# A delta-rule attention and SwiGLU kernel: the first group's triangular inverse by 16-row blocks, two to a partition, with TensorE turning rows and partitions

## The chip, the cores and the metric

The kernel runs on one core of one Trainium2 chip. The core has TensorE (PE, with its weight loads PEld), VectorE (DVE), ScalarE (ACT), GpSimd (POOL) and SyncE (SP, which here only issues DMAs). The metric is the device time of the whole program in microseconds, the median over several runs; lower is better.

## The reference

```python
B, H, S, D = 4, 8, 768, 48
k_n = k / (norm(k) + 1e-6)
for t in range(S):
    kt, vt, bt = k_n[:, :, t], v[:, :, t], beta[:, :, t, None]
    y[:, :, t] = einsum('bhd,bhde->bhe', q[:, :, t], state)
    v_old = einsum('bhde,bhd->bhe', state, kt)
    state += bt[..., None] * einsum('bhd,bhe->bhde', kt, vt - v_old)
x = y.transpose(0, 2, 1, 3).reshape(3072, 384)
out = (silu(x @ w_gate) * (x @ w_val)) @ w_out      # 384 -> 1536 -> 384
```

The first half is a recurrence over 768 steps for each of 32 pairs of batch and head; the second is a feed-forward block (FFN) over all 3072 tokens. The FFN's weights come as float64 and are converted on the chip.

## The kernel before

The sequence is cut into 12 chunks of C = 64 steps. Within a chunk the recurrence is solved in closed form: with A the strictly lower part of the products of K with itself, scaled by beta, the chunk's updates are the inverse of a unit triangular 64x64 matrix (times beta) applied to V minus what the state already holds. Such an inverse is needed for every chunk and each of the 32 pairs of batch and head. Two chunks make a group (6 groups).

The stages, with their functions:

- `norms(c)` (L299 to L326) normalizes K: a square and a sum on DVE (on POOL from chunk 2 on), a power 0.5 on POOL (L314), then an add, a reciprocal and a multiplication. It is a generator, and each `step` runs it to its next `yield`.
- `betas()` (L272) brings beta to partitions with 48 small PE products (p_b), ACT copies and one DVE transpose (L293).
- `turned(c, of_q)` (L328) turns K or Q by eight 128x128 PE transposes into two PSUM banks (p_t), and ACT copies all 1024 columns at once (L337).
- `gram(c, of_q)` (L341) makes the 64x64 products of K with K or with Q, 32 matmuls, and DVE copies them out of PSUM with one multiplication by a mask (L359), to a_sb or p_sb. K's mask also zeroes the upper right 32x32 block and gives the lower left one a minus sign.
- `invert(g)` (L377) inverts the 32x32 diagonal blocks: each of the 128 partitions holds one block, 1024 elements. `turn` (L366) moves a_sb into mb by DVE 32x32 transposes (L369, L372), L393 scales mb by minus beta, then 31 steps of a multiplication (L404, tmp) and an addition (L410, zb) run the substitution, zb is turned back into zt, and six more transposes make z1 (L425, L430).
- `join(g, chunks)` (L434) fills in the off-diagonal 32x32 block with two rounds of 32x32 PE products (p_j, L446 and L461), with an ACT copy between them (L452) and two copies into zt (L465, one on ACT and one on DVE).
- `advance(c)` (L474) uses zt, V and the state to produce the chunk's output and the next state, and turns the output for the FFN (x_ffn).
- `ffn(c, point, fill)` (L562) runs the FFN of a chunk's 256 tokens: six pairs of p_gate and p_val groups (L574), each followed by a silu on ACT (L583) and a product on DVE (L587), then two p_o groups (L595). `point` and `fill` put pieces of the next chunks' work between them.

`convert` (L166) makes float32 out of float64 words for one of 30 weight pieces: five DVE instructions (L178, L190, L199, L208, L217) and one on ACT (L186), which the fourth DVE instruction waits for. The pieces' loads run four ahead on SP's queue (`stage`, L149). `fill` (L702) issues conversions during chunk 0's FFN by a formula over the number done so far, and the rest of them after its last pair; only then do the invert steps of later groups go in.

The order of instructions on each engine is the order of the program text (`tc.manual_schedule`). L733 to L780 is that order: loads, norms of chunks 0 and 1, betas, K's and Q's transposes and products, all of `invert(0)`, then chunk 0's half of `join(0)` and `advance(0)`, with a conversion between every two steps, then the twelve FFN chunks. PSUM tiles come from `ps_pair` (tags px and py, two banks each, one buffer) and `ps_ffn` (tag ffn, four single banks); a tile of a tag waits until the one before it has been read.

Of the kernel before, what the change touches and what calls it, by code (L numbers as in the profile page):

```python
# [8 lines left out]
FP32 = mybir.dt.float32  # L9
# [5 lines left out]
C = 64  # L15
# [6 lines left out]
def kernel(  # L22
# [46 lines left out]
    def ps_pair(name, tag):  # L69

        return psum.tile([128, 2, 512], FP32, name=name, tag=tag, bufs=1)

    def ps_ffn(shape, name):
        return psum.tile(shape, FP32, name=name, tag="ffn", bufs=4)
# [159 lines left out]
    spare = const.tile([128, 1], FP32, name="spare")  # L234
    nc.scalar.activation(spare, half[:, 0:1], ACTF.Silu)


    mask_k = const.tile([128, C], FP32, name="mask_k")
    mask_q = const.tile([128, C], FP32, name="mask_q")
    for m in (mask_k, mask_q):  # L240
        nc.gpsimd.memset(m, 1.0)
        for b in range(2):
            rows = m[64 * b : 64 * b + 64]
            nc.gpsimd.affine_select(
                out=rows,
                in_=rows,
                compare_op=ALU.is_ge,
                fill=0.0,
                base=-1,
                pattern=[[1, C]],  # L250
                channel_multiplier=-1,
            )
    for b in range(2):
        nc.gpsimd.memset(mask_k[64 * b : 64 * b + R, R:C], 0.0)
        nc.gpsimd.memset(mask_k[64 * b + R : 64 * b + C, 0:R], -1.0)

    state = const.tile([128, 2, NB, NJ, D], FP32, name="state")
    beta_b = const.tile([128, NG, R], FP32, name="beta_b")
# [4 lines left out]
    def half_of(x):  # L263
        return slice(64 * x, 64 * x + 64)
# [34 lines left out]
    def norms(c):  # L299
# [25 lines left out]
            load_k(c + 2)  # L325
        yield  # L326

    def turned(c, of_q, tag=None):  # L328

        x = qpad[c % QB] if of_q else knp[c % AHEAD]  # L330
        xt = work.tile([128, NB, NJ, 2, C], FP32, name="qt" if of_q else "kt", bufs=AHEAD)
        (qt if of_q else kt)[c] = xt
        p_t = ps_pair("p_t", tag or ("py" if of_q else "px")).rearrange("p bp (j n) -> p bp j n", j=NJ)
        for bp in range(NB):
            for j in range(NJ):
                nc.tensor.transpose(p_t[:, bp, j], x[:, bp, 2 * j : 2 * j + 2], ident)  # L336
        nc.scalar.copy(xt.rearrange("p bp j b i -> p bp j (b i)"), p_t)  # L337
        if of_q and c + QB < NCH:
            load_q(c + QB)

    def gram(c, of_q, tag=None):  # L341

        xt = (qt if of_q else kt)[c]
        p_g = ps_pair("p_g", tag or ("py" if of_q else "px")).rearrange("p par (bp j i) -> p par bp j i", bp=NB, j=NJ)
        for bp, j, par, b, _ in every():
            nc.tensor.matmul(  # L346
                p_g[half_of(b if of_q else b ^ par), par, bp, j],
                kt[c][half_of(par), bp, j, b],
                xt[half_of(par), bp, j, b],
            )  # L350
        if of_q:
            p_sb[c] = work.tile([128, 2, NB, NJ, C], FP32, name="p_sb", bufs=AHEAD)
            dst = p_sb[c].rearrange("p par bp j i -> p (par bp j) i")
        else:
            g = c // 2
            if c % 2 == 0:
                a_sb[g] = work.tile([128, 2, HH, C], FP32, name="a_sb")
            dst = a_sb[g][:, c % 2]
        nc.vector.tensor_tensor(  # L359
            out=dst,  # L360
            in0=p_g.rearrange("p par bp j i -> p (par bp j) i"),
            in1=(mask_q if of_q else mask_k)[:, None, :].to_broadcast([128, HH, C]),
            op=ALU.mult,
        )

    def turn(out, in_):  # L366

# [6 lines left out]

    z1s = {}

    def invert(g):  # L377

        mb = work.tile([128, R, R], FP32, name="mb", bufs=1)
        zb = work.tile([128, R, R], FP32, name="zb", bufs=1)  # L380
        nc.gpsimd.memset(zb, 0.0)
        nc.gpsimd.tensor_copy(
            zb.rearrange("p k i -> p (k i)")[:, 0 : R * R : R + 1], beta_b[:, g]
        )
        nbeta = work.tile([128, R], FP32, name="nbeta")
        nc.gpsimd.tensor_scalar_mul(nbeta, beta_b[:, g], -1.0)
        a_v = a_sb[g].rearrange("p c h i -> p i (c h)")
        z_v = ztp[g % ZB].rearrange("p c h i -> p i (c h)")
        yield from turn(
            lambda rows, half: mb[rows].rearrange("p j i -> p i j"),  # L390
            lambda rows, half: a_v[rows, R * half : R * half + R],
        )
        nc.vector.tensor_tensor(  # L393
            out=mb,
            in0=mb,
            in1=nbeta[:, None, :].to_broadcast([128, R, R]),
            op=ALU.mult,
        )
        yield
        for j in range(R - 1):  # L400
            m = R - 1 - j
            tmp = work.tile([128, 256], FP32, name="tmp", bufs=1)
            t_v = tmp[:, 0 : (j + 1) * m].rearrange("p (k i) -> p k i", i=m)
            nc.vector.tensor_tensor(  # L404
                out=t_v,
                in0=zb[:, 0 : j + 1, j : j + 1].to_broadcast([128, j + 1, m]),
                in1=mb[:, j : j + 1, j + 1 : R].to_broadcast([128, j + 1, m]),
                op=ALU.mult,
            )
            nc.vector.tensor_tensor(  # L410
                out=zb[:, 0 : j + 1, j + 1 : R],
                in0=zb[:, 0 : j + 1, j + 1 : R],
                in1=t_v,
                op=ALU.add,
            )
            yield
        yield from turn(
            lambda rows, half: z_v[rows, R * half : R * half + R],
            lambda rows, half: zb[rows].rearrange("p k i -> p i k"),
        )  # L420

        z1 = work.tile([128, 2, NJ * NB, R], FP32, name="z1", bufs=1)
        zt = ztp[g % ZB].rearrange("p c (m e) i -> p c m e i", e=2)
        for c in range(2):
            nc.vector.transpose(z1[:, c], zt[:, c, :, 0, 0:R])  # L425
        yield
        for s in range(2):
            hi, lo = slice(64 * s, 64 * s + R), slice(64 * s + R, 64 * s + C)
            for c in range(2):
                nc.vector.transpose(z1[lo, c], zt[hi, c, :, 1, 0:R])  # L430
            yield
        z1s[g] = z1

    def join(g, chunks=slice(0, 2)):  # L434

        zt, a, z1 = ztp[g % ZB], a_sb[g], z1s[g]
        n = chunks.stop - chunks.start
        M = HH // 2
        p_j = ps_pair("p_j", "px")[:, 0].rearrange("p (c m i) -> p c m i", c=2, m=M)
        for c in range(chunks.start, chunks.stop):  # L440
            for m in range(M):
                for e in range(2):
                    for s in range(2):
                        lo = slice(64 * s + R, 64 * s + C)
                        dst = slice(64 * s + R * e, 64 * s + R * e + R)
                        nc.tensor.matmul(  # L446
                            p_j[dst, c, m],
                            a[lo, c, 2 * m + e, 0:R],
                            zt[lo, c, 2 * m + e, R:C],
                        )  # L450
        t2 = work.tile([128, 2, M, R], FP32, name="t2", tag="tmp", bufs=1)
        nc.scalar.copy(t2[:, chunks], p_j[:, chunks])  # L452
        yield
        p_j = ps_pair("p_j", "py").rearrange("p e (c m i) -> p e c m i", c=2, m=M)
        for c in range(chunks.start, chunks.stop):
            for m in range(M):
                for e in range(2):
                    for s in range(2):
                        row = slice(64 * s + R * e, 64 * s + R * e + R)
                        hi = slice(64 * s, 64 * s + R)  # L460
                        nc.tensor.matmul(p_j[hi, e, c, m], z1[row, c, m], t2[row, c, m])  # L461
        zt_v = zt.rearrange("p c (m e) i -> p e c m i", e=2)
        for s, copy in ((0, nc.scalar.copy), (1, nc.vector.tensor_copy)):
            hi = slice(64 * s, 64 * s + R)
            copy(  # L465
                zt_v[hi, :, chunks, :, R:C].rearrange("p e c m i -> p e (c m) i"),
                p_j[hi, :, chunks].rearrange("p e c m i -> p e (c m) i"),
            )
        yield
# [254 lines left out]
    with tc.manual_schedule(  # L724
# [13 lines left out]
        nc.gpsimd.memset(ztp[0], 0.0)  # L738
        for c in (0, 1):
            step("norm", norms, c)  # L740
        step("betas", betas)
        step("norm", norms, 0)
        turned(0, False)
        step("norm", norms, 1)
        turned(1, False, "py")
        step("betas", betas)
        gram(0, False)
        gram(1, False, "py")

        turned(0, True)  # L750
        turned(1, True)
        for _ in invert(0):
            pass
        gram(0, True)
        one = join(0, slice(0, 1))
        load_v(1)
        next(one)
        converts(1)
        next(one)
# [49 lines left out]
```

## Time and profile before

| | us |
|---|---|
| median of 3 runs (815.23 to 817.8) | 815.56 |
| profiled execution, whole | 817.87 |
| profiled execution, span | 816.2 |
| PE busy | 719.5 |
| PEld busy | 573.6 |
| DVE busy | 430.8 |
| ACT busy | 145.0 |
| POOL busy | 80.5 |
| first p_gate of the FFN starts at | 83.35 |
| last weight conversion ends at | 158.4 |

The span runs from the first to the last instruction of the profiled execution, and the positions in this text are microseconds from its start. An instruction's row in the order of time gives its start, its duration, the engine, the line, the operation, the tiles and shapes (partitions x elements), and in brackets how long the engine was idle before it and what ended the wait. A row with x2 merges several. A small float32 matmul appears as two records on PE and two weight loads on PEld, so x64 is 32 matmuls; a 128x128 transpose is one record. The granted clock is the share of PE's full clock that its throttle let through.

### The profile page before, as it was taken

Reading aid. Unit: us, or ns where it says so; the run is one execution under the profiler, and the core shown is the slowest. Engines: PE = TensorE matmul, PEld = TensorE weight load, DVE = VectorE, ACT = ScalarE, POOL = GpSimd, SP = SyncE. Lnnn points to the kernel's source line nnn. Section 1 sums busy time; section 2 is a strip of 40 time slices with the busy share of each in tenths; the row PEclk is TensorE's granted clock in tenths of the full one; section 3 lists DMA queues with packets and bytes.
Section 4 is the critical chain, followed back from the end, with each engine's and each line's share of the span. In section 5 each row is a group of like instructions: output and inputs, shape, how many; then the busy total and the mean of one; then the engine's idle time right before and its main releaser. Section 6 shows DMA issues by size and latency. Waiting matters only on the chain.

```text
span 816.2 us, 20536 instructions
## 1 busy us (share of the span) xinstructions
PE 719.5 (88%) x9384; PEld 573.6 (70%) x9384; DVE 430.8 (53%) x768; ACT 145.0 (18%) x230; POOL 80.5 (10%) x73
## 2 busy tenths in 40 slices
PE   3304868399989999999999999999999999999997
PEld 2303757268758877868868868868868778688784
DVE  3899799849824785207881157852277511011010
ACT  2003223311012111121201211211202111021110
POOL 6000032122003020030110121100000000000000
PEclk9655899599998999999999999999999999999999
DMA  8604564412013120120210211001001000000000
GB/s 192 110 1 105 174 174 110 132 31 50 0 25 58 22 49 12 22 49 15 44 23 12 40 31 31 2 21 22 2 20 22 2 21 2 10 12 1 19 1 19
DMA packets 85094, 34.45 MB, mean 42 GB/s; under 512 B 78064, under 2 KB 81136, under 8 KB 85008
## 3 DMA queue, kind: packets, MB, share of 16 engines
q1 hardware_dynamic: 79008, 27.93, 14.9%
q10 hardware_dynamic: 6000, 5.21, 2.7%
q8 instruction: 73, 1.20, 0.6%
q14 instruction: 13, 0.11, 0.0%
HBM read 28.41 MB, written 4.72 MB: 41 GB/s over the span
## 4 chain that ended last, share of the span: by engine, by line
PE 77%; DVE 15%; issue 4%; DMA 2%; POOL 1%; ACT 1%; ACTq 0%; POOLq 0%; DVEq 0%
PE p_gate L574 22%; PE p_o L595 21%; PE p_val L574 21%; PE p_g L346 2%; PE p_t L336 2%; DVE mant L199 2%; DVE power L208 2%; DVE zb L410 1%; DVE tmp L404 1%; PE p_u L505 1%; PE p_y L535 1%; DVE mant L190 1%; PE p_s L522 1%; PE p_r L484 1%; PE p_y L493 1%
## 5 line engine op out<-in xcount | busy, mean ns | idle before, releaser
L574 PE MATMUL p_gate<-x_ffn,wg_sb 128*128 128x256 f32 x864 | 205.7, 388 | 0.0
L574 PE MATMUL p_val<-x_ffn,wv_sb 128*128 128x256 f32 x864 | 198.7, 379 | 0.5 <-DVE wv_sb L217 0.5
L595 PE MATMUL p_o<-wo_sb,h_f 128*128 128x384 f32 x576 | 191.1, 490 | 0.0
L574 PEld LDWEIGHTS p_val<-x_ffn,wv_sb 128*128 128x128 f32 x864 | 164.0, 190 | 23.4 <-DVE wv_sb L217 1.2
L574 PEld LDWEIGHTS p_gate<-x_ffn,wg_sb 128*128 128x128 f32 x864 | 161.6, 192 | 23.6 <-DVE wg_sb L217 0.5
L587 DVE TENSOR_TENSOR h_f<-sil,p_val 128x512 f32<-128x512 f32 x72 | 49.3, 685 | 226.7 <-PE p_val L574 226.6
L595 PEld LDWEIGHTS p_o<-wo_sb,h_f 128*128 128x128 f32 x576 | 108.9, 191 | 72.7 <-issue 0.9
L583 ACT ACTIVATE sil<-p_gate 128x512 f32<-128x512 f32 x72 | 43.0, 597 | 211.2 <-PE p_gate L574 192.0
L410 DVE TENSOR_TENSOR zb<-zb,tmp 128x31 f32<-128x31 f32 (+15 forms) x186 | 68.5, 368 | 6.4
L404 DVE TENSOR_TENSOR tmp<-zb,mb 128x31 f32<-128x31 f32 (+15 forms) x186 | 67.8, 364 | 5.0
L314 POOL TENSOR_TENSOR norm<-norm,half 128x16 f32<-128x16 f32 x12 | 35.4, 2953 | 165.4 <-DVE norm L308 163.6
L603 ACT COPY o_sb<-p_o 128x384 f32<-128x384 f32 x24 | 11.5, 480 | 202.7 <-PE p_o L595 202.7
L318 POOL TENSOR_TENSOR kn<-kin,norm 128x768 f32<-128x768 f32 x10 | 14.8, 1479 | 293.6 <-DVE norm L317 246.6
L359 DVE TENSOR_TENSOR a_sb<-p_g,mask_k 128x1024 f32<-128x1024 f32 x12 | 14.7, 1223 | 45.2 <-PE p_g L346 45.2
L346 PE MATMUL p_g<-kt 64*64 64x64 f32 x768 | 16.1, 244 | 19.1 <-ACT kt L337 19.1
L446 PE MATMUL p_j<-zt,a_sb 32*32 32x32 f32 x768 | 8.3, 197 | 26.2 <-DVE zt L369 26.2
L346 PEld LDWEIGHTS p_g<-kt 64*64 64x64 f32 x768 | 14.5, 156 | 23.2 <-ACT kt L337 19.6
L186 ACT ACTIVATE power<-power,rebias 128x512 int32<-128x512 uint32 (+1 forms) x30 | 19.9, 677 | 58.4 <-DVE power L178 56.2
L446 PEld LDWEIGHTS p_j<-zt,a_sb 32*32 32x32 f32 x768 | 7.5, 108 | 28.8 <-issue 28.7
L372 DVE STREAM_TRANSPOSE zt<-zb 32x1024 f32<-32x1024 f32 x12 | 26.3, 2188 | 0.1
L372 DVE STREAM_TRANSPOSE mb<-a_sb 32x1024 f32<-32x1024 f32 x12 | 25.6, 2136 | 0.3
L465 DVE COPY zt<-p_j 32x1024 f32<-32x1024 f32 (+1 forms) x7 | 7.5, 1070 | 32.3 <-ACT zt L465 32.2
(85 smaller groups left out, 548.1 us busy)
## 6 DMA issues: line engine op xcount, KB each, us to landing
wo_sb<-in_moe_w_gate_dram SPq DMA_DIRECT2D x9, 512.0 KB, 3.6
wo_sb<-in_moe_w_val_dram SPq DMA_DIRECT2D x9, 512.0 KB, 3.8
qpad<-in_q_dram SPq DMA_DIRECT2D x48, 96.0 KB, 3.0
vin<-in_v_dram SPq DMA_DIRECT2D x96, 48.0 KB, 2.4
out_dram<-o_sb ACTq DMA_DIRECT2D x48, 96.0 KB, 2.2
kin<-in_k_dram SPq DMA_DIRECT2D x44, 96.0 KB, 2.9
staged<-in_moe_w_out_dram SPq DMA_DIRECT2D x6, 384.0 KB, 3.2
zt<-in_moe_w_out_dram SPq DMA_DIRECT2D x6, 384.0 KB, 3.6
```

Source lines behind the costliest of these rows:

```text
L186: nc.scalar.activation(power.bitcast(I32), power, ACTF.Relu, bias=rebias, scale=8.0)
L199: nc.vector.scalar_tensor_tensor(out=mant.bitcast(FP32), in0=words[:, :, 0], scalar=2.0**-32, in1=mant, op0=ALU.mult, op1=ALU.add,)
L208: nc.vector.scalar_tensor_tensor(out=power, in0=words[:, :, 1], scalar=0x80000000, in1=power, op0=ALU.bitwise_and, op1=ALU.bitwise_or,)
L314: nc.gpsimd.tensor_tensor(out=norm, in0=norm, in1=half, op=ALU.pow)
L346: nc.tensor.matmul(p_g[half_of(b if of_q else b ^ par), par, bp, j], kt[c][half_of(par), bp, j, b], xt[half_of(par), bp, j, b],)
L372: nc.vector.transpose(out(rows, 0), in_(rows, 0))
L404: nc.vector.tensor_tensor(out=t_v, in0=zb[:, 0 : j + 1, j : j + 1].to_broadcast([128, j + 1, m]), in1=mb[:, j : j + 1, j + 1 : R].to_broad ...
L410: nc.vector.tensor_tensor(out=zb[:, 0 : j + 1, j + 1 : R], in0=zb[:, 0 : j + 1, j + 1 : R], in1=t_v, op=ALU.add,)
L574: nc.tensor.matmul(ps[name][:, i], w_sb[:, t, (f + i) * 128 : (f + i + 1) * 128], x[:, t], start=(t == 0), stop=(t == KT - 1),)
L583: nc.scalar.activation(sil, ps[name], ACTF.Silu)
L587: nc.vector.tensor_tensor(out=hs[-1][:, f % 4 : f % 4 + 2], in0=sil, in1=ps["p_val"], op=ALU.mult)
L595: nc.tensor.matmul(p_o, hs[f // 4][:, f % 4, bp * 128 : (bp + 1) * 128], wo_sb[:, f], start=(f == 0), stop=(f == FT - 1),)
```

## The change

Only the first group is treated anew; `invert` remains for groups 1 to 5.

- The new `invert_first(0)` takes the place of `invert(0)`. a_sb reaches mb by 128 small PE products with the identity (p_m) and one DVE multiplication out of PSUM. The diagonal blocks are of 16 rows, two of them side by side in each partition, so the substitution has 15 steps in place of 31. PE turns the blocks back twice (p_z, as they are needed in zt, and p_d, as weights), 16x16 off-diagonal blocks come from two rounds of 128 PE products (p_j), and PE makes z1 (p_1) in place of DVE's transposes.
- `between(n)` puts other work into it: a weight conversion beside p_m (n = 0), Q's transposes and chunk 0's product with Q (n = 1), that product's masks (n = 2), and a conversion each at n = 3 and 4. Before, Q's transposes and product stood around `invert(0)`, and its mask followed it.
- K's mask is gone: K's products are copied as they are (on DVE; chunk 1's on ACT), and the minus sign is put in by `join`'s ACT instruction instead (`scalar.mul` by -1).
- `turned` and `gram` now work with single banks: each copy out of PSUM is two of half the size, in every chunk.
- The two steps of chunk 0's `norms` run before those of chunk 1, on DVE too.
- mb and zb are 1056 elements wide (were 1024). `join(0)`'s first half swaps its PSUM tags. `load_v(1)` is issued ahead of Q's second loads.

```diff
-    mask_k = const.tile([128, C], FP32, name="mask_k")
...
+            nc.scalar.copy(xt[:, bp].rearrange("p j b i -> p (j b i)"), p_t[bp])
...
+            else:
+                at = slice(par * HH // 2, (par + 1) * HH // 2)
+                copy(a_sb[c // 2][:, c % 2, at], p_h)
...
+    def invert_first(g, between):
+        mb, zb, nbeta = blocks(g)
+        a, zt = a_sb[g], ztp[g % ZB]
+        a_v, z_v = (t.rearrange("p c h i -> p (c h) i") for t in (a, zt))
...
+        for j in range(R):
+            for quad, at in QUADS:
+                nc.tensor.matmul(
+                    p_m[quad, R * j : R * j + R], a_v[quad, :, at + j], ident[quad, quad]
+                )
+        between(0)
+        nc.vector.tensor_tensor(
+            out=mb[:, 0 : R * R].rearrange("p (j i) -> p j i", i=R),
+            in0=p_m.rearrange("p (j i) -> p j i", i=R),
+            in1=nbeta[:, None, :].to_broadcast([128, R, R]),
+            op=ALU.mult,
+        )
+        between(1)
+        r = R // 2
...
+        for j in range(r - 1):
+            m = r - 1 - j
+            shape = [128, 2, j + 1, m]
...
+            nc.vector.tensor_tensor(
+                out=t_v,
+                in0=z_h[:, :, 0 : j + 1, j : j + 1].to_broadcast(shape),
+                in1=m_h[:, :, j : j + 1, j + 1 : r].to_broadcast(shape),
+                op=ALU.mult,
+            )
+            done = z_h[:, :, 0 : j + 1, j + 1 : r]
+            nc.vector.tensor_tensor(out=done, in0=done, in1=t_v, op=ALU.add)
...
+        for i in range(R):
+            for quad, _ in QUADS:
+                nc.tensor.matmul(
+                    p_z[quad, R * i : R * i + R], z_t[quad, :, i], ident[quad, quad]
+                )
+        between(2)
+        for n, (quad, at) in enumerate(QUADS):
+            (nc.scalar.copy if n < 2 else nc.vector.tensor_copy)(
+                z_v[quad, :, at : at + R],
+                p_z[quad].rearrange("p (i h) -> p h i", h=2 * HH),
+            )
...
+                nc.tensor.matmul(
+                    p_d[quad, R * k : R * k + R], z_t[quad, k], ident[quad, quad]
+                )
...
+        nc.scalar.copy(d_v, p_d)
...
+                nc.tensor.matmul(
+                    p_j[quad, h],
+                    a_v[quad, h, at : at + R],
+                    z_v[quad, h, at + r : at + R],
+                )
...
+        nc.scalar.mul(t1, p_j, -1.0)
+        between(3)
...
+                nc.tensor.matmul(p_j[quad, h], d_v[quad, h], t1[quad, h])
+        for n, (quad, at) in enumerate(QUADS):
+            rows = slice(quad.start, quad.start + r)
+            (nc.scalar.copy if n % 2 == 0 else nc.vector.tensor_copy)(
+                z_v[rows, :, at + r : at + R], p_j[rows]
+            )
+        between(4)
...
+                        nc.tensor.matmul(
+                            p_1[dst, c, m], zt[hi, c, 2 * m + e, 0:R], ident[hi, hi]
+                        )
+        z1s[g] = work.tile([128, 2, HH // 2, R], FP32, name="z1", bufs=1)
+        nc.scalar.copy(z1s[g], p_1)
...
-        nc.scalar.copy(t2[:, chunks], p_j[:, chunks])
+        nc.scalar.mul(t2[:, chunks], p_j[:, chunks], -1.0)
...
         for c in (0, 1):
             step("norm", norms, c)
+            step("norm", norms, c)
         step("betas", betas)
-        step("norm", norms, 0)
         turned(0, False)
-        step("norm", norms, 1)
         turned(1, False, "py")
         step("betas", betas)
         gram(0, False)
-        gram(1, False, "py")
-
-        turned(0, True)
-        turned(1, True)
-        for _ in invert(0):
-            pass
-        gram(0, True)
-        one = join(0, slice(0, 1))
+        gram(1, False, "py", nc.scalar.copy)
         load_v(1)
+
+        first_q = gram_steps(0, True, "ffn")
+
+        def between(n):
+            if n == 1:
+                for c in range(2):
+                    turned(c, True, "ffn")
+                next(first_q)
+            elif n == 2:
+                next(first_q)
+            else:
+                converts(1)
+
+        invert_first(0, between)
+        one = join(0, slice(0, 1), ("py", "px"))
```

## The prediction

> **What bounds the kernel now.** I read the page's first three parts, then sums over stretches of the span, then the instructions in order of time up to 190 us. The page:
>
> ```profile
> PE 719.5 (88%) x9384; PEld 573.6 (70%) x9384; DVE 430.8 (53%) x768; ACT 145.0 (18%) x230; POOL 80.5 (10%) x73
> PE   3304868399989999999999999999999999999997
> DVE  3899799849824785207881157852277511011010
> PEclk9655899599998999999999999999999999999999
> ```
>
> Over the whole span PE is the bound; in the first eight slices of 20.4 us it is not, and DVE is. The stretches (length, then PE, PEld, DVE, ACT, POOL busy, granted clock, DMA share, GB/s) say it in numbers:
>
> ```profile
> 24.24:65.40 41.16, 6.12 (x144) 5.19 (x144) 38.70 (x77) 2.40 (x3) 1.47 (x1) 0.53 0.27 48
> 65.35:158.40 93.05, 57.91 (x999) 49.51 (x1002) 87.31 (x169) 31.94 (x51) 11.52 (x6) 0.78 0.53 152
> 160.40:816.20 655.80, 644.39 (x7940) 508.95 (x7932) 293.54 (x508) 106.45 (x168) 53.05 (x39) 0.99 0.11 21
> ```
>
> From 24.2 to 65.4 only DVE works (the first group's inverse). From 65.4 to 158.4 DVE is 94% busy, with the 30 weight conversions. From 160.4 on PE is 98% busy. So the time is about (end of the conversions) + 658, and the end of the conversions is DVE's own sum. DVE time taken out ahead of it moves everything behind it. The first group, in order of time:
>
> ```profile
> 24.26 2.14 DVE L369 STREAM_TRANSPOSE mb<-a_sb 128x1024 f32<-128x1024 f32 x1
> 26.44 4.25 DVE L372 STREAM_TRANSPOSE mb<-a_sb 32x1024 f32<-32x1024 f32 x2
> 30.80 1.23 DVE L393 TENSOR_TENSOR mb<-mb,nbeta 128x1024 f32<-128x1024 f32 x1
> 32.05 0.19 DVE L404 TENSOR_TENSOR tmp<-zb,mb 128x31 f32<-128x31 f32 x1
> ...
> 43.26 0.43 DVE L404 TENSOR_TENSOR tmp<-zb,mb 128x256 f32<-128x256 f32 x1
> ...
> 55.41 2.18 DVE L369 STREAM_TRANSPOSE zt<-zb 128x1024 f32<-128x1024 f32 x1
> 57.49 4.31 DVE L372 STREAM_TRANSPOSE zt<-zb 32x1024 f32<-32x1024 f32 x2
> 57.74 1.08 PE L446 MATMUL p_j<-zt,a_sb 32*32 32x32 f32 x64 [26.20 <-DVE zt L369]
> 61.84 0.77 DVE L425 STREAM_TRANSPOSE z<-zt 128x256 f32<-128x256 f32 x2
> 62.64 1.54 DVE L430 STREAM_TRANSPOSE z<-zt 32x256 f32<-32x256 f32 x4
> 64.21 1.23 DVE L359 TENSOR_TENSOR p_sb<-p_g,mask_q 128x1024 f32<-128x1024 f32 x1
> 68.19 0.69 DVE L465 COPY zt<-p_j 32x512 f32<-32x512 f32 x1
> ```
>
> No idle stands between the DVE rows up to 65.4; the last row, at 68.9, completes chunk 0's inverse, with one conversion behind it of 30.
>
> **The change, step by step.** Times are of the profiled execution (span 816.2, whole 817.87; the median of the runs is 815.56). I sum a saving there and take it off the median.
>
> 1. Norms. Chunk 1's square and sum now stand behind chunk 0's power on DVE. Chunk 0's normalized K is ready 1.6 us earlier, which helps nobody, as PE takes both chunks in order. Chunk 1: chunk 0's power ends at 10.39, then 0.16 + 0.25 + 0.96 on DVE, square and sum 1.9, to 13.85, against 12.1 before. So +1.75, and K's products end at 24.7, not 22.93. The copies out of PSUM lose the mask; chunk 1's go to ACT as two halves (0.57 each by a 128x512-like row; half of kt's 1.01 is the other end), against one 1.23 pass on DVE. a_sb is ready at **25.95** (before 24.23).
>
> 2. Rows to partitions: 128 matmuls of 32x32 in place of 6.5 us of transposes. The only 32x32 rows are p_b (48 in 1.50) and p_j: 32 (64 records) in 1.08, or 33.8 ns each, at granted clock 0.5, and 0.75, or 23.4 ns, at 79.6 us. PE has worked from 19 us on here, and in the old trace the 128x128 transposes go from 1.97 to 1.09 us per eight after such a stretch (24.3 us), so 23.4: 3.0 us (cold 4.3). The first conversion runs on DVE beside it. Scaling from PSUM 1.23 (L359's row), and 0.5 (0 to 1.2) for GpSimd's 1.47 us square, which lands at 28.6 as before and has delayed DVE's two-operand rows by about 1.2 us elsewhere (L404 at 188.2 took 1.45). To **30.75**.
>
> 3. The recurrence: 30 instructions, not 62. From the rows, start to start is 0.20 us + 1.02 ns per element (0.23 at 31, 0.46 at 256). The new ones hold 2720 elements: 6.0 + 2.8 = 8.8 us, where 23.4 were. Their four-dimensional views I cost at nothing: the old 1-wide and 31-wide forms take the same 0.2. Q's transposes, copies and product now run on PE and ACT beside the loop (3 to 6 us, ample cover of 8.8). To **39.55**.
>
> 4. Blocks back. 60 of p_z's 128 matmuls go with the loop; 68 are behind it, cold, 2.3 us: 41.85. Q's masks (1.4) hide here. Four 32x1024 copies: two on ACT (1.01), then two on DVE (1.22), one behind the other, since the instruction order shows DVE's wait for ACT: 46.4. Side by side they would end at 44.3, with PE then late at 45.55. PE's p_d (128, 3.7) and ACT's copy of it hide there. They read PSUM 32 elements apart; L369 reads 64 apart at 2.1 ns an element, where the contiguous L293 transpose takes 1.9, so I add nothing, and up to half of 4.5 as the other end.
>
> 5. Joining halves: p_j 128 matmuls 3.2 to 49.65, t1 0.65 to 50.3, the second 128 3.3 to 53.6, four 16-row copies in turn (0.57, 0.69, twice, with 0.05 each) to **56.3**.
>
> 6. Then DVE has two conversions (68.91 to 71.65: 2.74 each) ahead of its zt copy: 61.85, and 62.55 with the copy. p_1 (64 matmuls, 1.9), z1 and join's two products on PE end at 60.2 and ACT's copy at 60.8: covered. Without that cover, slower PE shows at once, 1 for 1.
>
> So zt is whole at 62.55, not 68.88: **6.3 us earlier**. And four conversions are behind it, not one (one beside p_m, one beside the joining, two after): three times 2.74 is 8.2. Until the first p_gate the stages are the same. In the first FFN pairs DVE still decides: PE waits there for p_sb (101.15), wg_sb (104.76), wv_sb (108.09), and the fill's formula then issues three conversions in the first four fills in place of six. DVE's wait of 3.3 us at 86.3 (ACT's L186 stands behind sil, which waits for the first p_gate) stays. Walking pairs 0 to 3 with these rows, DVE comes 7 to 8.8 us sooner to chunk 1's update, counted from the first p_gate; I take **8.0**. The rest to 158.4 and PE's 658 shift unchanged.
>
> Other edits at nothing: later groups' copies as two halves add some 0.15 us per tile to ACT and DVE, both under half busy from 160 us on, where PE is the cover; bounds -1 and +1 us. V's loads now issue ahead of Q's second ones on SP's queue; Q's chunks 2 and 3 are first read past 135 us. GpSimd loses mask work that was done by 4.5 us.
>
> Sum: 6.3 + 8.0 = 14.3; 815.56 - 14.3 = **801.3**.
>
> **A rule that speaks against it.** The weights of p_m, p_z and the second joining product are read 32 or 64 elements apart, 324 such matmuls on the path; every stationary operand in this trace is contiguous, so nothing shows what that costs. The nearest rows give 23.4 (no cost) and twice that (the 64-column p_u, 61 ns cold against 33.8): +7.6 us. I take nothing, as the record count and the width, which set those rows, are the same. The Trainium skill, "SBUF — State Buffer", section "Door 1: The DMA port swizzle", says that fp32 read further than four elements apart leaves its 16-byte line each time and pays for it. It gives no figure; by it the step would be dearer, and by the rows it is free.
>
> **Rivals.**
> - *Strided weights cost double*: 14.3 - 7.6 = 6.7, **808.9**. For it: nothing measured. Against it: L369's 2.1 ns is on DVE, not PE. 10%.
> - *The three hidden conversions are worth nothing*, because PE becomes the bound in the first FFN chunk: only 6.3 stays, **809.3**. For it: PE is 15 of 20 us busy from 100 to 120. Against it: 35 us of PE idle in the 93, 18 of them at one wait at 156.84. 8%.
> - *More*: PE warm throughout, copies side by side (-2.2) and the first p_gate, 5.0 us at 83.4, at the 2.86 of the next, for which DVE now waits 3.3: **797**. 9%.
> - *Slower*: strided weight loads do not overlap the matmul ahead of them. Place: those 324; price: one PEld record of 104 ns (L446's median) in place of 30, +24 us, so **825**. It decides from about 75 ns a matmul on (14.3/324 = 44 more). For it: no row excludes it. Against it: PEld busy is 0.97 of 1.08 us for 64 records, so loads are pipelined. 5%.
> - *It moves nothing*: the weight transfers bound the tail. The last pieces land 0.7 us (153.71 against 154.38) ahead of use, so a slightly later transfer would show, but DVE waits for none today: 815, 2%.
> - The forecast: 66%.
>
> **Numbers.** All cold PE adds 3.4, strided copies 2.3, the later stages 1: 14.3 - 6.7 = 7.6, or 808. The other ends give 797, and 795 with everything. I set 796 to 810, which takes in all but the last two cases and the edge of the others. Faster by over 0.3% (2.4 us, about what a measurement here can tell from no change): 66 + 10 + 8 + 9 = 93%; within 2%; slower 5%.
>
> **What would show it.** Right: DVE's loop near 9 us and ending near 40; the group of 128 matmuls at 3 to 4.3 us; zt whole near 62.5 with three further conversions done; conversions ending near 144; from there 658. Wrong: 128-matmul groups at 6 us or more (strided), a PE stall between the copies, DVE waiting for ACT or PE between 80 and 144, or a PE-bound part longer than 659.

## The result

The changed kernel takes **838.72 us** (median of 4 runs, 836.01 to 846.47) against 815.39 for the kernel before: ratio 1.0296, 95% interval 1.0225 to 1.0367. That is slower by 3%, where 801.3 was forecast, and it lies outside the range of 796 to 810. The profiled execution took 838.62, its span 836.9.

The page of the changed kernel, the lines that answer to those shown of before:

```profile
PE 746.9 (89%) x10792; PEld 595.2 (71%) x10792; DVE 406.3 (49%) x750; ACT 155.1 (19%) x263; POOL 80.0 (10%) x66
PE   2754886489988999989999999999999999999997
DVE  3535899748833876216883137761186711011010
PEclk9855799599998999999999999999999999999999
```

DVE lost 24.5 us of busy time, as intended. In slices 2 to 4 (20.9 to 83.7 us) it is no longer full; PE is not either. The two stretches that matter, in the same columns as in the prediction (length, then PE, PEld, DVE, ACT, POOL busy, granted clock, DMA share, GB/s). The weight conversions end at 158.67 us, as good as unchanged (158.35 before). The first row is the first group of the changed kernel, the second its stretch behind the conversions, the third that same stretch before the change:

```profile
26.00:65.00 39.00, 24.85 (x1259) 22.45 (x1260) 17.60 (x44) 8.18 (x12) 1.76 (x1) 0.65 0.37 72
158.80:836.90 678.10, 653.12 (x8064) 513.45 (x8064) 295.82 (x529) 110.49 (x188) 55.09 (x40) 0.99 0.11 21
158.35:816.20 657.85, 646.44 (x8016) 510.94 (x8008) 294.77 (x510) 106.45 (x168) 55.10 (x40) 0.99 0.11 21
```

In the first one DVE works 17.6 of 39 us and PE 24.9: the stage is now a chain in which each waits for the other. The stretch behind the conversions was 657.85 us before and had been carried over "unchanged". Counted from 158.67 (the row starts 0.13 behind it) it is 678.2, **20.4 longer**, with only 6.7 more PE busy time. So there are two misses, and they add up. Within the profiled executions the forecast was 817.87 - 14.3 = 803.6; the conversions end 14.6 later than the 144.05 that this meant, the rest takes 20.4 more, and 803.6 + 35.0 = 838.6, the time of the profiled execution.

**Miss one, the later stage.** Each turning of K or Q is eight transposes, four into each of the two PSUM banks of one tile. PE in order of time, the turning of K and Q in the changed kernel (chunk 6; start, duration, what runs, in brackets the wait ahead of it):

```profile
300.73 0.60 PE L338 MATMUL p_t<-ident,kn 128*128 128x128 f32 x4
302.00 0.66 PE L338 MATMUL p_t<-ident,kn 128*128 128x128 f32 x4 [0.68 <-ACT kt L339]
302.50 0.60 PE L338 MATMUL p_t<-ident,qpad 128*128 128x128 f32 x4
303.82 0.66 PE L338 MATMUL p_t<-ident,qpad 128*128 128x128 f32 x4 [0.73 <-ACT qt L339]
304.32 7.91 PE L715 MATMUL p_o<-wo_sb,h_f 128*128 128x384 f32 x24
```

and the same place before:

```profile
292.27 1.04 PE L336 MATMUL p_t<-ident,kn 128*128 128x128 f32 x8
293.14 1.04 PE L336 MATMUL p_t<-ident,qpad 128*128 128x128 f32 x8
294.01 7.91 PE L595 MATMUL p_o<-wo_sb,h_f 128*128 128x384 f32 x24
```

From the first transpose to p_o it was 1.74 us and is 3.59. ACT's copy of bank 0 now stands between the two fours, and the second four, which write bank 1 of the same tile, wait for it. Six of the ten later chunks lose 1.85 each, 11.1. Chunks 5 and 7 lose 2.6 and 3.1 (in chunk 7 the wait for ACT's copy is 1.91, not 0.68). Chunks 2 and 3, whose transposes stand elsewhere, lose 3.3 and 2.0: chunk 2's p_g starts at 160.42, not 156.84, of which 0.3 is the later end of the conversions, and chunk 3 takes 5.0 from p_t to p_g, not 3.0. The sum is 22.1, 1.7 more than the 20.4 by which the stage is longer; e5 shows a gain of about that size.

**Miss two, the first group.** PE there, the rows of p_m and then from the first product of p_d on:

```profile
27.05 3.83 PE L413 MATMUL p_m<-ident,a_sb 32*32 32x32 f32 x238 [1.19 <-ACT a_sb L370]
32.83 0.52 PE L413 MATMUL p_m<-ident,a_sb 32*32 32x32 f32 x18 [1.95 <-issue]
...
45.36 0.63 PE L462 MATMUL p_d<-ident,zb 32*32 32x32 f32 x28
47.35 1.93 PE L462 MATMUL p_d<-ident,zb 32*32 32x32 f32 x128 [1.36 <-issue]
51.35 1.54 PE L462 MATMUL p_d<-ident,zb 32*32 32x32 f32 x98 [2.07 <-issue]
...
54.95 1.90 PE L472 MATMUL p_j<-zt,a_sb 32*32 32x16 f32 x128 [1.71 <-issue]
58.41 1.57 PE L472 MATMUL p_j<-zt,a_sb 32*32 32x16 f32 x101 [1.55 <-issue]
60.68 0.63 PE L483 MATMUL p_j<-t,mb 32*32 32x16 f32 x27 [0.70 <-ACT t L478]
62.14 2.01 PE L483 MATMUL p_j<-t,mb 32*32 32x16 f32 x128 [0.83 <-issue]
67.24 1.66 PE L483 MATMUL p_j<-t,mb 32*32 32x16 f32 x101 [3.09 <-issue]
```

Within a row of p_d or p_j a product (two records) takes 30 ns, near the 25 to 29 that these terms were priced at. Between the rows PE stands for 0.8 to 3.1 us, and "issue" says that nothing in the profile released it. From p_d on the rows break every 128 records, right across the steps (28, 128, then 98 of p_d and some 27 of p_j, 128, and so on); p_m ran 238 records before its one pause. 64 products are 128 matmul records and 128 weight loads. The page's part on queues has the answer, queue q8, with packets, MB and share:

```profile
q8 instruction: 84, 1.38, 0.7%
```

1.38 MB in 84 packets is 16.4 KB each; over the 256 instructions of such a row that is 64 bytes each. The counts of whole runs agree: PE and PEld together have 2 x 10792 instructions, which is 84.3 times 256, and before the change 2 x 9384, which is 73.3 times 256, for 73 packets. In the trace of packets one starts 1.0 to 1.7 us after each of these rows has begun in most cases (2.8 us in the row ahead of the longest pause), takes about 0.95 us, and PE resumes 1.3 to 1.5 us after its end. So a burst of small products runs at the pace at which its instructions are brought in: about 3.5 us for 64 products, 54 ns each, not 30.

### The profile page after: what moved, and what is told of

Read it like the earlier page. It is cut to its first block, busy times and chain, and to the rows that moved or that the text cites. A ratio compares the mean times of both kernels' runs of the same rounds, so it can differ in the third digit from the quotient of the medians.

```text
span 836.9 us, 23384 instructions
## 1 busy us (share of the span) xinstructions
PE 746.9 (89%) x10792; PEld 595.2 (71%) x10792; DVE 406.3 (49%) x750; ACT 155.1 (19%) x263; POOL 80.0 (10%) x66
## 3 DMA queue, kind: packets, MB, share of 16 engines
q8 instruction: 84, 1.38, 0.7%
## 4 chain that ended last, share of the span: by engine, by line
PE 78%; DVE 10%; issue 6%; ACT 3%; POOL 2%; DMA 1%; ACTq 0%; POOLq 0%; DVEq 0%
PE p_gate L694 22%; PE p_o L715 21%; PE p_val L694 20%; PE p_g L349 2%; PE p_t L338 2%; DVE mant L199 2%; DVE power L208 2%; PE p_u L625 1%; PE p_y L613 1%; PE p_s L642 1%; PE p_r L604 1%; PE p_y L655 1%; ACT kt L339 1%; DVE mant L190 1%; POOL norm L308 1%
## 5 line engine op out<-in xcount | busy, mean ns | idle before, releaser
L530 DVE TENSOR_TENSOR zb<-zb,tmp 128x31 f32<-128x31 f32 (+15 forms) x155 | 57.9, 374 | 5.3
L524 DVE TENSOR_TENSOR tmp<-zb,mb 128x31 f32<-128x31 f32 (+15 forms) x155 | 57.1, 369 | 3.9
L338 PE MATMUL p_t<-ident,kn 128*128 128x128 f32 x96 | 18.0, 318 | 34.4 <-ACT kt L339 28.9
L370 DVE COPY a_sb<-p_g 128x512 f32<-128x512 f32 x22 | 14.2, 685 | 56.4 <-PE p_g L349 56.4
L338 PEld LDWEIGHTS p_t<-ident,kn 128*128 128x128 f32 x96 | 12.5, 160 | 39.7 <-ACT kt L339 32.0
L338 PE MATMUL p_t<-ident,qpad 128*128 128x128 f32 x96 | 17.4, 318 | 7.2 <-ACT qt L339 7.2
L621 DVE TENSOR_TENSOR vin<-vin,p_r 128x768 f32<-128x768 f32 x11 | 10.5, 954 | 24.0 <-PE p_r L604 23.6
L383 DVE STREAM_TRANSPOSE zt<-zb 32x1024 f32<-32x1024 f32 x10 | 22.0, 2197 | 0.1
L383 DVE STREAM_TRANSPOSE mb<-a_sb 32x1024 f32<-32x1024 f32 x10 | 21.4, 2136 | 0.3
```

What stands on the lines that cost most here:

```text
L338: nc.tensor.transpose(p_t[bp][:, at], x[:, bp, 2 * j : 2 * j + 2], ident)
L383: nc.vector.transpose(out(rows, 0), in_(rows, 0))
L524: nc.vector.tensor_tensor(out=t_v, in0=zb[:, 0 : j + 1, j : j + 1].to_broadcast([128, j + 1, m]), in1=mb[:, j : j + 1, j + 1 : R].to_broad ...
L530: nc.vector.tensor_tensor(out=zb[:, 0 : j + 1, j + 1 : R], in0=zb[:, 0 : j + 1, j + 1 : R], in1=t_v, op=ALU.add,)
```

## The experiments

Kernels measured together share the runs of the kernel before, whose median lay at 815.5 to 816.2 us.

**e1: both copies behind all eight transposes.** The changed kernel with one line more:

```diff
                 nc.tensor.transpose(p_t[bp][:, at], x[:, bp, 2 * j : 2 * j + 2], ident)
+        for bp in range(NB):
             nc.scalar.copy(xt[:, bp].rearrange("p j b i -> p (j b i)"), p_t[bp])
```

> The changed kernel, but in every chunk both half copies of K's and Q's transposes come after all eight transposes, not one between the two fours. Theory A (the copy in the middle makes PE wait before the second four, since the second bank's transposes wait for the reading of the first): the waits of PE for kt and qt inside the transposes go. In the trace of the changed kernel K's and Q's transposes of a later chunk take 3.59 us together where they took 1.74 before, 1.85 us for each of ten chunks, so about 838.7 - 18.5 = 820. Rival (the half-size copies of the products on DVE, or more ACT instructions, make the later stage longer): no change, 837 to 840. Theory B (the first group's gain is eaten by PE waiting for its instructions): what is left over the kernel before is the first group's, so not under 814.

Measured: 815.18 (10 runs) against 815.88, ratio 0.9992 [0.9972, 1.0012]: 23.5 us less than the changed kernel. PE no longer waits inside the eight, and the rest behind the conversions is 654.3 us:

```profile
290.04 1.04 PE L338 MATMUL p_t<-ident,kn 128*128 128x128 f32 x8
290.91 1.04 PE L338 MATMUL p_t<-ident,qpad 128*128 128x128 f32 x8
```

```profile
159.60:813.90 654.30, 644.23 (x8020) 509.32 (x8012) 295.85 (x530) 107.66 (x186) 55.26 (x40) 1.00 0.11 22
```

The place of the copy, not its halving, costs the time. That it fell below the expected 820 is mostly the reckoning: 18.5 was ten times 1.85, and the ten turnings had cost 22.1. The conversions still end at 159.6: miss two is untouched.

**e2: the split alone.** The kernel before, with one half copy inside the loop, and nothing else of the change:

```diff
                 nc.tensor.transpose(p_t[:, bp, j], x[:, bp, 2 * j : 2 * j + 2], ident)
-        nc.scalar.copy(xt.rearrange("p bp j b i -> p bp j (b i)"), p_t)
+            nc.scalar.copy(xt[:, bp].rearrange("p j b i -> p (j b i)"), p_t[:, bp])
```

> The kernel before with one edit: the copy of the transposes is split into two halves, each after its four transposes, as in the change. Theory A: ten chunks by 1.85 us in the later stage and up to 2 more in the first, so 815.4 + 18.5 = 834 (832 to 838). Rival (the split itself is harmless, something else of the change made the later stage longer): 815 to 817.

Measured: 841.64 against 815.88, 1.0297 [1.0273, 1.0322]. This one line alone is enough for the whole slowdown; the length behind the conversions (from 157.1 us) is 680.4:

```profile
157.10:837.50 680.40, 654.59 (x8065) 514.30 (x8064) 294.67 (x510) 110.51 (x188) 55.13 (x40) 0.99 0.11 21
```

It is more than the 832 to 838 expected, which again reckoned 1.85 for each chunk. The stretch is 2.3 longer than in the changed kernel, which has the products' copies split as well (e5).

**e10: the same two fours into two tiles.** Why does bank 1 wait for a copy of bank 0? In the changed kernel, K's fours of the later chunks get a tile each; Q's stay as they are:

```diff
-        p_t = banks("p_t", tag or ("py" if of_q else "px"))
+        if c > 1 and not of_q:
+            p_t = [ps_pair("p_t0", "px")[:, 0], ps_pair("p_t1", "py")[:, 0]]
+        else:
+            p_t = banks("p_t", tag or ("py" if of_q else "px"))
```

> The changed kernel with one edit: from chunk 2 on, K's two fours of transposes write two separate PSUM tiles (bank 0 of tag px, bank 0 of tag py) in place of the two banks of one tile; Q's stay in one tile. If the wait between the fours comes from the tile being one object (theory), K's second four follows the first at once in all ten later chunks (no wait for the kt copy inside K's eight, which now take about 1.04 us), while Q's fours still wait 0.7 us in eight chunks; Q's first four, whose tile now follows K's second one, may wait instead until ACT has read it (about 0.7 us), so the whole time is not the point and may stay at 836 to 840. If the wait comes from PSUM itself (PE kept out while ACT reads), K's second four still waits 0.68 us.

Measured (one run): 841.8, and at the same place:

```profile
302.17 1.04 PE L341 MATMUL p_t<-ident,kn 128*128 128x128 f32 x8
303.94 0.66 PE L341 MATMUL p_t<-ident,qpad 128*128 128x128 f32 x4 [0.73 <-ACT kt L342]
305.27 0.66 PE L341 MATMUL p_t<-ident,qpad 128*128 128x128 f32 x4 [0.68 <-ACT qt L342]
```

K's eight run through; Q's, in one tile, still wait in the middle (and once more ahead, because their tile is now the one that K's second four used). So the wait belongs to the tile, which is one object however many banks it has: the instructions are made to wait for each other by tile, and PSUM itself does not keep PE out. The first group's Q in the changed kernel says the same: its halves are two tiles of the ffn tag, and its 16 transposes run in one row of 3.00 us. The Trainium skill, "PSUM — Partial Sum Buffer", section "PSUM bank collisions raise a hardware error", states that two engines on different banks do not collide and that guarding by bank is enough; these rows agree, since ACT's copy of one tile's bank (from 302.81 on) and PE's writes to the other's (up to 303.21) ran side by side here.

**e3: bursts of small products, measured by themselves.** The kernel before with three bursts of 256 products behind its last: 32 columns with contiguous weights, 32 columns with weights 12 elements apart, 128 columns.

```diff
+        b_w = wo_sb[:, 0].rearrange("p (a b) -> p b a", b=12)
+        for kind in range(3):
+            p_x = ps_pair("p_x" + str(kind), ("px", "py", "px")[kind])[:, 0]
+            for i in range(256):
+                quad = slice(32 * (i % 4), 32 * (i % 4) + 32)
+                if kind == 1:
+                    w = b_w[quad, i // 4 % 12]
+                else:
+                    w = wo_sb[quad, i // 4 % 12, 0:32]
+                n = 128 if kind == 2 else 32
+                nc.tensor.matmul(p_x[quad, 0:n], w, ident[quad, 0:n])
```

> The kernel before with three bursts of 256 PE products added behind its last one, which nothing reads: 32x32 weights contiguous, 32 columns moving; the same with weights read 12 elements apart; 32x32 weights contiguous with 128 columns moving. The data transfers are nearly over by then. Theory B (small products use up instructions faster than they are brought: 128 records, with their loads 256 instructions, per block of 16 KB): the first two bursts run alike, in stretches of 128 records at 23 to 34 ns a product with a pause of 1.3 to 2 us between that has no releaser, about 3.5 us per 64 products; the third, at some 200 ns a product, has no pause. Rival (strided weights load slower): the second burst is slower than the first within the stretches, by 20 ns a product or more. Rival (PSUM or row groups pace the products): no pauses, but 50 ns or more a product in both.

Measured (one run, 860.31; the burst begins with a row of 153 records at 813.70, so the first two rows below and most of the third are contiguous weights, the last two are strided ones):

```profile
817.45 1.64 PE L790 MATMUL p_x<-ident,wo_sb 32*32 32x32 f32 x128 [2.26 <-issue]
821.19 1.93 PE L790 MATMUL p_x<-ident,wo_sb 32*32 32x32 f32 x128 [2.11 <-issue]
824.66 1.99 PE L790 MATMUL p_x<-ident,wo_sb 32*32 32x32 f32 x128 [1.54 <-issue]
828.13 2.41 PE L790 MATMUL p_x<-ident,wo_sb 32*32 32x32 f32 x128 [1.48 <-issue]
832.15 2.39 PE L790 MATMUL p_x<-ident,wo_sb 32*32 32x32 f32 x128 [1.61 <-issue]
```

The same pauses, 1.35 to 2.26 us after every 64 products, with nothing to wait for and next to no data on the DMA queues. The start-to-start time is 3.5 to 4.0 us. The strided weights show too: 2.39 against 1.93 us a row, 37 against 30 ns a product, at a granted clock of 0.50 in both. That is a quarter more of the busy part, and from row to row 3.7 to 4.0 us where the contiguous rows had 3.5 to 3.7; the rival as put, 20 ns a product or more, falls. The burst of 128 columns shows no pauses but at its beginning. Its products take 64 ns each, not the 200 expected, so 64 of them last 4.1 us, about as long as a packet takes to come.

**e4: 64 products fewer.** e1, but of p_d only the half that is read (and the second joining product with 16 columns of weights):

```diff
-        for k in range(R):
+        for k in range(r):
...
-                nc.tensor.matmul(p_j[quad, h], d_v[quad, h], t1[quad, h])
+                rows = slice(quad.start, quad.start + r)
+                nc.tensor.matmul(p_j[rows, h], d_v[quad, h], t1[quad, h])
```

> The first of these experiments (both copies after the transposes), and p_d halved: only the 16 columns that the second joining product uses are turned, 64 products fewer, and that product has 16 columns of weights, with the same result. Theory B: 64 products fewer are one block of instructions fewer on the path, 3.5 us, while DVE's work is the same; the inverse is whole 3.5 us earlier, and the total, where DVE waits for PE in the first group, drops by 3 to 4 us against that experiment. Rival (the products cost their 30 ns): 1.9 us less. If DVE and not PE sets the end of the first group: no change.

Measured: 810.82 against 815.88, 0.9927 [0.9903, 0.9951]; 4.4 below e1. The joining starts at 48.85, not 52.7, and zt is whole at 74.54, not 79.75. Of these 5.2 us 1.5 stand ahead of p_d, where the two kernels are alike (43.84 against 45.36); the other 3.7 are about one packet's period, where 30 ns each would give 1.9. The run also has one packet less, 83 for 84. But one pause grew to 4.38 us. A weight piece's load had been issued just before, and the next instruction packet started only 3.2 us after PE had resumed.

**e8: that load out of the burst.** e4 with the conversion at n = 3, and with it the load, moved to n = 4:

```diff
-                converts(1)
+                for _ in range({0: 1, 3: 0, 4: 2}[n]):
+                    converts(1)
```

> The halved p_d kernel (810.8), with the conversion that ran beside the second joining product moved behind it, so that no weight load is issued while those products run (the end of a conversion issues the next load on SP's queue, at 57.1 there). The question is what makes one pause of PE's instruction supply 4.4 us (before the last 102 records of that product) where the others are 1.0 to 2.0. Theory B with the weight load in the way of the fetch: that pause falls to about 2 us, and the product ends some 2.4 us sooner after its start. Rival (the long pause belongs to the fetch itself, by its place in the program): it stays at 4.4 us. The total should stay within 2 us of 810.8, since the moved conversion now stands ahead of DVE's zt copy.

Measured: 809.47 (2 runs) against 816.05, 0.9917 [0.9886, 0.9948], so e4's time within the uncertainty. The pause in question, first in e4, then in e8:

```profile
62.89 1.04 PE L485 MATMUL p_j<-t,mb 32*16 32x16 f32 x102 [4.38 <-issue]
```

```profile
62.02 1.04 PE L485 MATMUL p_j<-t,mb 32*16 32x16 f32 x102 [2.74 <-issue]
```

The pause is 1.6 us shorter without the load, but that the load makes the difference is not shown: e6 issues one 0.13 us behind the start of the same row (57.08 against 56.95), and its pause there is 2.19. With one profile of each kernel, what sets the length of this pause stays open.

**e5: the products' masked copies in halves.** The kernel before, with the DVE copy of K's and Q's products in two halves:

```diff
-        nc.vector.tensor_tensor(
-            out=dst,
...
+        p_h = p_g.rearrange("p par bp j i -> p (par bp j) i")
+        for par in range(2):
+            at = slice(par * HH // 2, (par + 1) * HH // 2)
+            nc.vector.tensor_tensor(
+                out=dst[:, at],
+                in0=p_h[:, at],
...
```

> The kernel before with one edit: the masked copies of K's and Q's products out of PSUM are two DVE instructions of 512 columns, not one of 1024, as in the change (the masks stay). Theory A (only the split inside the transposes makes PE wait; here all products are issued before the first copy): no change, 814 to 818. Rival (splitting the copies costs by itself, DVE's or PSUM's): a part of the 20 us that the later stage of the changed kernel is longer, over 818.

Measured: 813.71 against 816.18, 0.9975 [0.9963, 0.9986]. Not a cost but a gain of about 2.5 us. In the profile the conversions end 1.6 earlier (156.72 against 158.35), and the rest takes 656.0, 1.9 less than before. That is of the size of the 2.3 by which the later stage is shorter in the changed kernel than in e2, and of the 1.7 by which the losses of its ten turnings exceed what the stage is longer. Why the halves are faster stays open, and so does what else makes e1's 654.3.

**e6: DVE's free time filled.** e4, with the conversions spread so that DVE has work wherever PE is slow (a slot n = 5 ahead of p_d is new), and at least one conversion in each fill of the first FFN chunk, where the formula's least was none at first and one later:

```diff
-                converts(1)
+                for _ in range({0: 2, 3: 3, 4: 1, 5: 2}[n]):
+                    converts(1)
...
-            for _ in range(max(-(-(upto - due) // (4 - n % 4)), n // 8)):
+            for _ in range(max(-(-(upto - due) // (4 - n % 4)), 1)):
```

> The halved p_d kernel (810.8), with more weight conversions where DVE is idle in the first group: two beside p_m (one more), two behind the copies of p_z (new), three while the joining products run (two more), and then one per fill in chunk 0's FFN at the least. Nothing else. Theory B (the first group's end is set by PE's instruction supply, DVE waits there): DVE does five conversions more before chunk 0's inverse is whole, at no cost to PE; the conversions' end, and with it PE's 17.8 us wait for kt ahead of p_g, moves forward until PE's own work of chunk 0's FFN sets it: 810.8 - 12 = 799 (795 to 803). Rival (DVE's sum bounds the first stage, as the prediction had it): moving conversions changes nothing, 809 to 813. If the weight loads delay the instruction fetches, pauses between stretches of products grow from 1.5 to 3 us or more and up to 6 us of the gain go.

Measured: 799.06 against 816.18, 0.9792 [0.9769, 0.9816], as expected. The conversions end at 141.4 us, and PE's wait for them is down to 9.64 (17.8 in e1):

```profile
139.78 1.99 PE L350 MATMUL p_g<-kt 64*64 64x64 f32 x64 [9.64 <-ACT kt L340]
```

**e7 and e9: the old order of the norms.** e6 with the norms' steps in the old order (the 1.75 us of the prediction's first step), and that once more with `{0: 2, 3: 2, 4: 2, 5: 2}`.

> The kernel with more conversions, and the order of chunks 0 and 1 in the norms as before the change: chunk 1's square and sum ahead of the wait for chunk 0's power. The prediction's step 1 (K's products end 1.75 us later by the new order, and PE's chain is the bound of the first group): 1.75 us less than the run beside it. If the chain is not the bound there: no change.

> The kernel with more conversions and the old norm order, with one conversion moved from beside the joining products to behind them, so that DVE's last copy into zt does not wait behind a conversion (PE waited 2.1 us for it at p_1 in the kernel with three there). If that wait is all that the third one costs: 0 to 2 us less than 799, say 798. If DVE's sum or the fetches bound the stage: no change, 797 to 801.

Measured: 799.10 against 816.18, 0.9789 [0.9769, 0.9809], and 798.70 against 816.05, 0.978 [0.9756, 0.9803]. In e7 p_m starts 2.5 us sooner than in e6 (23.03 against 25.51), but the pauses in the second joining product grow from 0.76 and 2.19 to 2.41 and 2.74, and chunk 0's p_u starts at 72.70 against 72.65. So in these two profiles the 2.5 us given to a chain that waits for its instructions were not kept. e9's 798.7 fits both of its expected outcomes and decides nothing. e6, e7 and e9 are 2.1 to 2.2% below the kernel before and cannot be told from each other.

## Why the prediction was wrong

Step by step, forecast against the changed kernel's trace:

| step | forecast | measured |
|---|---|---|
| 1, a_sb ready | 25.95 | 26.99 |
| 2, p_m (128 products) | 3.0 us | 6.3 us |
| 3, recurrence | 8.8 us | 8.64 us |
| 4, p_z behind the loop; four copies in turn | 2.3; 4.5 us | 2.16; 4.53 us |
| 4, p_d (128) | 3.7, hidden | 7.5, of which 2.5 show |
| 5, p_j twice (128 each) | 3.2; 3.3 us | 7.3; 8.2 us |
| 5, inverse joined | 56.3 | 71.6 |
| 6, zt whole | 62.55 | 78.56 (68.88 before) |
| conversions end | about 144 | 158.7 |
| from there on | 658 us | 678.2 us |

- **The step that decided the sign** is "other edits at nothing: later groups' copies as two halves ... where PE is the cover; bounds -1 and +1 us". It counted ACT's and DVE's instructions (0.15 us a tile) and took PE as the engine that hides them. It did not ask which PE instruction stands behind the first half copy. PE did not cover the copy, it waited for it: the stage is 20.4 us longer. e2 (that line alone, +25.8), e1 (that line undone, -23.5) and e10 (the wait goes with the tile) show it.
- **The other failed terms** are the 128-product ones of steps 2, 4 and 5. They were priced by rows of 32 products, which fit into half a packet of instructions, and the sum has no term for the supply of instructions. p_m, p_d and the two p_j came to 3.3, 2.5, 4.1 and 4.9 us more; a_sb adds 1.0 (K's own second four wait there as well: in e1 it is ready at 25.9), the other steps -0.5, together the 15.3 by which the joining is late. Of p_m's 3.3 the pause is 1.95; the rest is the products themselves, 32 ns each at a granted clock of 1.00, where p_j's row at 79.6 us, by which they were priced, gave 23.4. The trace of before had the warning in small: behind 24 of the 64 records of p_r, at 237 us, PE stood for 1.61 us with "issue" as its reason. e3 shows the pauses without any of the change, e4 that fewer products shorten the chain by more than their own time, about a packet's.
- **The saving on DVE was right and then not cashed.** Four conversions stand behind the first group, not one, as forecast (8.2 us). From zt to the conversions' end it takes 80.1 us, 9.4 less than before, where 8.0 had been taken. But zt is whole 9.7 us later than before, not 6.3 sooner, and the two cancel: the conversions end where they did. e6 is the counterproof: with miss one mended, miss two in part and DVE's idle time filled they end at 141.4, and the time is 799. That this is near the 801.3 forecast for the change itself is luck: zt is whole at 72.6 there, not at 62.55, and it is five more conversions ahead of it that make up for this.
- **The rivals.** Strided weights at double cost fell: 7 ns more a product in e3, and in the second p_j, whose weights lie 32 apart, 2.01 us a row against 1.90 in the first. p_m's 32 ns for 23.4, with weights 64 apart, may be such a cost, 1.1 us in all; no run isolates it. "Three hidden conversions worth nothing" fell with e6. The slower rival had the right sign by luck: it put 24 us on the PE chain, which was 15.3 late, but its mechanism, weight loads that do not overlap, is not what the rows show, as inside a row 30 ns a product hold. Two of the signs of being wrong came true: groups of 128 products took 6 us or more, though not for their strides, and the PE-bound part was longer than 659. No case priced a wait in the later stage or in the supply of instructions, and so the range ended at 810.

## What to carry to other kernels

Before a copy is cut in two, look at what stands next on the engine that writes the tile: a copy between two halves of its writes makes the second half wait, however many banks the tile has, so put the copies behind all writes, as in e1, or give each half a tile that nothing else needs at once (in e10 K's second tile was Q's next one, the wait moved there, and the whole gained nothing). A long chain of small matmuls is paid by its instructions, not by its columns. Bursts here ran 76 products (e3) and 119 (p_m) before their first pause and then 64 at a time, so price a longer one by the 54 to 62 ns of a long burst, not by the 30 ns of a short one, and cut the number of products first. Where work moves off the bounding engine onto a slower chain, the freed time is worth something only when other work of that engine is put into it.

## What the runs showed of the hardware

- PE's instructions came in packets of 16.4 KB while the program ran (84 in the changed kernel, 73 before, 85 in e3, 83 in e4, each time the number of PE's and PEld's instructions over 256). A packet holds 64 small float32 products; in most cases a long burst went at 3.5 to 4.0 us a packet, with pauses of 0.8 to 3.1 us. The Trainium skill, "Trainium Architecture — The Big Picture", section "The software stack", says that the instruction streams are moved to the engines when the program is loaded; by these rows at least a part of them comes during the run.
- A 512 KB load issued in such a burst went with a pause of 4.38 us in e4 and of 2.19 in e6; without a load the pause was 2.74 (e8). What the load does to it is not shown.
- Weights read 12 elements apart took 37 ns a product, contiguous ones 30, both at a granted clock of 0.50.
